# Attention ahead of two expert layers on one core: a per-engine order worked out in the source and chained, tiles 0 and 1 in one step, coefficients loaded later

## The chip, the cores and the metric

One core of a Trainium2 chip runs the whole program. The metric is the device time of one execution in microseconds (us). The engines are TensorE (PE, with PEld for its weight loads), VectorE (DVE), ScalarE (ACT), GpSimd (POOL) and SyncE (SP), which issues the loads and stores.

## What is computed

Causal attention for 2 batches and 12 heads over 448 tokens with heads of 64 wide, then an expert layer with a rational activation, then a gated one:

```python
def _attn_ref(q, k, v):
    ...
    scores = scale * np.matmul(q, k.transpose(0, 1, 3, 2))
    scores = np.where(mask, -1000000000.0, scores)
    scores = scores - np.max(scores, axis=-1, keepdims=True)
    attn = np.exp(scores)
    attn = attn / (np.sum(attn, axis=-1, keepdims=True) + 1e-09)
    return np.matmul(attn, v).astype(np.float32)

def _moe_ref(x, w_in, w_out, a, b):
    h = x @ w_in
    P = a[0] + a[1] * h + a[2] * h2 + a[3] * h3
    Q = 1.0 + np.abs(b[0]) * np.abs(h) + np.abs(b[1]) * h2
    g = P / (Q + 1e-06)
    return (g @ w_out).astype(np.float32)

def _moe2_ref(x, w_gate, w_val, w_out):
    gate = 1.0 / (1.0 + np.exp(-(x @ w_gate)))
    val = x @ w_val
    return (gate * val @ w_out).astype(np.float32)
```

x has 896 tokens (448 of each batch) by 768. w_in is 768 by 2048, w_out of the first layer 2048 by 768, the weights of the second 768 by 1536 and back. q, k and v are float32; the weights come as float64.

## The kernel before

**Attention.** Two heads of one batch make a pair, so there are 12 pairs, n = 0 to 11, 0 to 5 of batch 0. The 448 queries of a pair are four tiles t = 0 to 3 of 112 rows, and tile t meets t + 1 key tiles. For each tile: `scores` (L334) on PE for both heads into a PSUM slot "s"; `maxima` (L342) on VectorE masks, scales and takes the row maximum; `exps` (L358) on ScalarE; `turn` (L374) on PE transposes the exponentials into another slot "s" (called p); `copied` brings them to memory, on ScalarE for t = 2 (L381), else on VectorE (L383). At the pair's last tile `inverses` (L365, L366) inverts the row sums, `values` spreads them on PE (r, L395) and multiplies by v (x, L404), `result` (L416, L417) multiplies both, and `parts` splits the result into xh (L424, ScalarE) and xl (L427, GpSimd, or VectorE for the last pair of a batch). The pool of "s" has two slots, shared by s and p; x and r have one bank each, and two banks "mm" are left for the expert layer.

**Products of the expert layers.** Each product of full precision is three matmuls: high by high, high by low, low by high part. `weight` makes the parts of a weight: a load of 768 KB into "raw" (L117), two ScalarE steps (L126, L129), one VectorE step to "val" (L132), a ScalarE cast (L137, the high part) and a GpSimd subtraction (L139, the low part). raw and val have two buffers each. The first layer runs over four chunks of four tiles of 128 hidden values. h<c>_<b>_<i> is tile i of chunk c for batch b, 18 matmuls in `up` (L185, L187, L189); `rational` then makes its parts gh (L214, ScalarE) and gl (L216, GpSimd) by way of z, d and t (ScalarE L197 to L199, L207, L208; VectorE L201 to L203, L210 to L212). o<c>_<b>_<e> is tile e of the six output tiles, 12 matmuls in `out1` (L288, L290, L292), added into y by `sum1`.

**The order.** A loop over 48 steps (n, t) with a look-ahead of three (L474) emits the stages of attention, each at raised priority (`ahead`), and puts pieces of other work between them: two products each from a list of fillers (`products`), the steps of the first weights (`fetch`), and the rest of the rationals (`tick`). The framework's scheduler then fixes the order on each engine. h0_0_0 and h0_0_1 go in pair by pair as x gets ready (`early`), h0_0_2, h0_0_3 and o0_0 in the second half (`FILL_AT`). After attention its memory is released, and the chunks follow in a fixed sequence: h0_1, then for each chunk the next weights, next h and o. The loads of pairs 0 and 1, then those of the coefficients a and b, stand first on SP, and the negated b first on VectorE:

```python
    load(0)
    load(1)
    nc.sync.dma_start(out=a_sb, in_=ca.unsqueeze(0).to_broadcast([P, 4]))
    nc.sync.dma_start(out=b_sb, in_=cb.unsqueeze(0).to_broadcast([P, 2]))
    nc.vector.tensor_scalar_mul(nb, b_sb, -1.0)
    nc.vector.tensor_tensor(nb, nb, b_sb, op=ALU.min)
```

Of the kernel before, what the change touches and what calls it, by code (L numbers as in the profile page):

```python
# [26 lines left out]
def _run(g):  # L27
    while not _spent(g):
        pass


@with_exitstack
def tile_causal_attention__moe_rational__moe_glu(
# [74 lines left out]
    last = {}  # L108

    def paced(engine):  # L110

        return tc.issue_after(last[engine].ins) if engine in last else nullcontext()

    def weight(hi, lo, src, nm):
# [11 lines left out]
        nc.scalar.activation(w_f, w_f, AF.Prelu, scale=2.0**-112, alpha=2.0**32)  # L126

# [3 lines left out]
        with paced("dve"):  # L131
            nc.vector.scalar_tensor_tensor(  # L132
                val, w_hi, 3, w_lo, op0=ALU.logical_shift_left, op1=ALU.bitwise_or
            )
# [24 lines left out]
    NF = 4  # L159
# [32 lines left out]
    def rational(ps, gh, gl, nm):  # L192
# [12 lines left out]
        yield  # L205
# [30 lines left out]
    def early(k, after):  # L236

        for i in range(2):
            nm = f"h0_0_{i}"
            if k == 0:  # L240
                if i == 0:
                    gh = g_a.tile([P, 2, S], F32R, tag="gh", name=f"gh_{nm}")
                    gl = g_a.tile([P, 2, S], F32R, tag="gl", name=f"gl_{nm}")
                else:
                    gh, gl = g["e"]
                g["e"] = gh, gl
                g[0, 0, i] = (gh[:, i], gl[:, i])
                g["p", i] = psum_tile(nm)
            yield from up(g["p", i], wi[0][0], i * P, 0, [k])
            if k == KC - 1:  # L250
                after(rational(g["p", i], *g[0, 0, i], nm))

    def in1(c, b, after, i0=0):

        for i in range(i0, NF):
            nm = f"h{c}_{b}_{i}"
            if i % 2 == 0:
                pool = gpools[(c * B + b) % 2]
                gh = pool.tile([P, 2, S], F32R, tag="gh", name=f"gh_{nm}")
                gl = pool.tile([P, 2, S], F32R, tag="gl", name=f"gl_{nm}")  # L260
            g[c, b, i] = (gh[:, i % 2], gl[:, i % 2])
            ps = psum_tile(nm)
            yield from up(ps, wi[c][i // 2], (i % 2) * P, b)
            after(rational(ps, *g[c, b, i], nm))
# [14 lines left out]
    def out1(c, b, after):  # L279
        if c == 0:  # L280
            y1.append(ypools[b].tile([P, YW], F32, tag="y", name=f"y1_{b}"))
        for e in range(KC):
            es = slice(e * P, (e + 1) * P)
            ps = psum_tile(f"o{c}_{b}_{e}")
# [9 lines left out]
            after(sum1(ps, c, b, e))  # L294
# [7 lines left out]
    st = att.enter_context(tc.tile_pool(name="st", bufs=6))  # L302
# [5 lines left out]
    steps = [(n, t) for n in range(len(pairs)) for t in range(NQ)]  # L308
    T = {}

    PK = NQ - 1
    NB = PK * PK + NQ

    def load(n):
# [37 lines left out]

    def exps(n, t):
        d = T[n]
        sc = d["sc", t]
        for j in range(2):
            e = d["e", t, j]
            nc.scalar.activation(  # L358
                e, e, AF.Exp, bias=sc[:, j : j + 1], scale=-1.0, accum_out=d["sum"][:, t, j : j + 1]
            )  # L360

    def inverses(n, t):
        if t == NQ - 1:
# [21 lines left out]
    def values(n, t):  # L385

        if t < NQ - 1:
            return
        d = T[n]
        d["r"] = ps_r.tile([P, 512], F32, tag="r", name=f"r_{n}")[:, :S]  # L390
        d["x"] = ps_x.tile([P, 512], F32, tag="x", name=f"x_{n}")[:, :S]

        for i in range(NQ):
            for j in range(2):
# [6 lines left out]
                )  # L401
        for kt in range(NQ):
            for j in range(2):
                last["pe"] = nc.tensor.matmul(  # L404
                    d["x"][j * D : (j + 1) * D, kt * CP :],
                    d["v"][:, kt, j],
                    d["pt"][:, j, kt * (PK + 1) : kt * PK + NQ].rearrange("p k c -> p (k c)"),
                    start=(kt == 0),
                    stop=(kt == NQ - 1),
                )  # L410

    def result(n, t):
        if t == NQ - 1:
            d = T[n]
            xn = d["xn"] = xn_p.tile([P, S], F32, tag="xn", name=f"xn_{n}")
            nc.scalar.copy(xn, d["r"])  # L416
            nc.vector.tensor_tensor(xn, xn, d["x"], op=ALU.mult)  # L417

    def parts(n, t):
        if t == NQ - 1:  # L420
            b, hp = pairs[n]
            x = (slice(None), hp, slice(b * S, (b + 1) * S))
            xn = T[n]["xn"]
            nc.scalar.copy(xh[x], xn)  # L424

            eng = nc.vector if hp == NP - 1 else nc.gpsimd
            eng.tensor_tensor(xl[x], xn, xh[x], op=ALU.subtract)  # L427
            del T[n]

    side = []  # L430
    queue = deque()
    loading = []
    fill = deque()
    held = []

    def ahead(offset=50):
        return tc.high_priority(offset=offset)

    def tick():
        for s in list(side):  # L440
            if _spent(s):
                side.remove(s)

    def fetch():
        if not loading and queue:
            loading.append(queue.popleft())
        if loading and _spent(loading[0]):
            loading.clear()

    def products():  # L450
        with paced("pe"):
            k = 4 if held and fill and fill[0] is held[0] else 1
            while k > 0 and fill and not (held and fill[0] is held[0] and side):
                if _spent(fill[0]):
                    fill.popleft()
                else:
                    k -= 1

    def stage(f, i):
        if 0 <= i < len(steps):  # L460
            with ahead():
                f(*steps[i])

    ns = len(steps)
    LA = 3
    AHEAD = 4
    IN_AT, OUT_AT, FILL_AT = 4, 14, ns // 2 + 1
    load(0)
    load(1)
    nc.sync.dma_start(out=a_sb, in_=ca.unsqueeze(0).to_broadcast([P, 4]))  # L470
    nc.sync.dma_start(out=b_sb, in_=cb.unsqueeze(0).to_broadcast([P, 2]))
    nc.vector.tensor_scalar_mul(nb, b_sb, -1.0)
    nc.vector.tensor_tensor(nb, nb, b_sb, op=ALU.min)
    for i in range(-LA, ns + 1):  # L474
        m, off = divmod(i + LA + AHEAD, NQ)
        if off == 3 and 1 < m + 1 < len(pairs):
            load(m + 1)
        if i == IN_AT:
            queue.extend(load_in(0))

# [3 lines left out]
        if i == OUT_AT:  # L484
            queue.extend(load_out(0))
# [182 lines left out]
```

## Time and profile before

| what | value |
|---|---|
| median of 3 runs | 663.45 us (663.27 to 663.7) |
| the profiled execution, its own time | 663.94 us |
| its span, first to last instruction | 662.2 us |
| mean granted clock of PE, share of 2.4 GHz | 0.969 |
| busy: PE, PEld, DVE, ACT, POOL | 94%, 81%, 58%, 57%, 36% |
| loaded and stored | 65 MB, 97 GB/s over the span |

The profile is of one execution. An engine's busy share is a mean over stages that differ: attention, up to about 175 us, is made of many small steps on four engines, and what follows is mostly long runs of matmuls. So the stage is read first, and in it what PE waits for, since an engine that is idle without anyone waiting for it costs nothing. A row of the timeline gives start, duration, engine, line, written<-read tile, the number of instructions joined, and in brackets the idle time before it with what ended it. The names there leave out the numbers: "h" is any h tile.

### The profile page before, as it was taken

Reading aid. Unit: us, or ns where it says so; the run is one execution under the profiler, and the core shown is the slowest. Engines: PE = TensorE matmul, PEld = TensorE weight load, DVE = VectorE, ACT = ScalarE, POOL = GpSimd, SP = SyncE. Lnnn points to the kernel's source line nnn. Section 1 sums busy time; section 2 is a strip of 40 time slices with the busy share of each in tenths; the row PEclk is TensorE's granted clock in tenths of the full one; section 3 lists DMA queues with packets and bytes.
Section 4 is the critical chain, followed back from the end, with each engine's and each line's share of the span. In section 5 each row is a group of like instructions: output and inputs, shape, how many; then the busy total and the mean of one; then the engine's idle time right before and its main releaser. Section 6 shows DMA issues by size and latency. Waiting matters only on the chain.

```text
span 662.2 us, 8797 instructions
## 1 busy us (share of the span) xinstructions
PE 623.8 (94%) x3352; PEld 534.1 (81%) x3352; DVE 386.8 (58%) x659; ACT 380.0 (57%) x712; POOL 237.8 (36%) x155
## 2 busy tenths in 40 slices
PE   5888688999898999999999989999999999999997
PEld 3555355577697888999999879899999999999997
DVE  2656658843489899998978964222433454222314
ACT  3677878844397988869638848565544424310110
POOL 0132402110255464262245779433614334220100
PEclk7779979999998999999999989999999999999999
DMA  6262641100054155123006345352322504100004
GB/s 222 86 215 87 215 149 46 42 15 1 1 191 143 49 159 175 49 60 131 0 5 195 136 130 173 126 191 76 115 96 95 191 1 150 42 1 0 1 1 166
DMA packets 25641, 65.05 MB, mean 98 GB/s; under 512 B 1984, under 2 KB 3776, under 8 KB 25600
## 3 DMA queue, kind: packets, MB, share of 16 engines
q1 hardware_dynamic: 25600, 64.50, 29.7%
q8 instruction: 26, 0.43, 0.3%
q14 instruction: 15, 0.12, 0.1%
HBM read 61.74 MB, written 2.75 MB: 97 GB/s over the span
## 4 chain that ended last, share of the span: by engine, by line
PE 61%; DVE 15%; ACT 10%; issue 5%; DMA 4%; POOL 4%; SPq 0%; DVEq 0%; ACTq 0%; POOLq 0%
PE z L598 4%; PE z L599 4%; PE z L600 4%; PE vu L185 4%; PE gu L185 4%; PE gu L189 4%; PE vu L189 4%; PE gu L187 4%; PE vu L187 4%; PE s L334 3%; PE h L185 3%; PE p L374 3%; PE o L288 3%; PE h L187 3%; PE o L292 3%
## 5 line engine op out<-in xcount | busy, mean ns | idle before, releaser
L185 PE MATMUL h<-xh,wh_in 128*128 128x448 f32 x192 | 71.4, 377 | 6.8 <-ACT xh L424 5.0
L288 PE MATMUL o<-gh_h,oh 128*128 128x448 f32 x192 | 69.2, 377 | 5.7 <-DVE t_h L203 3.9
L586 POOL TENSOR_TENSOR gl<-pr_u,gh 128x448 fp32r<-128x448 f32 x24 | 28.4, 1183 | 127.0 <-ACT gh L585 127.0
L290 PE MATMUL o<-gl_h,oh 128*128 128x448 f32 x192 | 72.2, 376 | 1.5 <-POOL gl_h L216 1.4
L187 PE MATMUL h<-xl,wh_in 128*128 128x448 f32 x192 | 71.5, 373 | 1.5 <-POOL xl L427 1.5
L292 PE MATMUL o<-gh_h,ol 128*128 128x448 f32 x192 | 71.4, 372 | 0.0
L189 PE MATMUL h<-xh,wl_in 128*128 128x448 f32 x192 | 70.8, 370 | 0.0
L216 POOL TENSOR_TENSOR gl_h<-t_h,gh_h 128x448 fp32r<-128x448 f32 x32 | 45.1, 1412 | 61.9 <-ACT gh_h L214 48.7
L358 ACT ACTIVATE e<-e,sc 112x112 f32<-112x112 f32 (+3 forms) x96 | 50.0, 524 | 28.9 <-DVE sc L342 28.8
L342 DVE CUSTOM_DVE_ANT_0 e<-s,mask 112x112 f32<-112x112 f32 (+3 forms) x96 | 39.1, 446 | 33.8 <-PE s L334 33.2
L582 DVE TENSOR_TENSOR pr_u<-sg_u,vu 128x448 f32<-128x448 f32 x24 | 14.8, 617 | 73.3 <-PE vu L189 54.5
L598 PE MATMUL z<-oh_z,gh 128*128 128x384 f32 x168 | 56.3, 335 | 0.0
L599 PE MATMUL z<-ol_z,gh 128*128 128x384 f32 x168 | 56.2, 334 | 0.0
L600 PE MATMUL z<-oh_z,gl 128*128 128x384 f32 x168 | 56.2, 334 | 0.0
L185 PE MATMUL gu<-xh,wh_gt 128*128 128x448 f32 x144 | 53.0, 368 | 0.7 <-ACT sg_u L581 0.7
L185 PE MATMUL vu<-xh,wh_vl 128*128 128x448 f32 x144 | 53.1, 369 | 0.0
L189 PE MATMUL vu<-xh,wl_vl 128*128 128x448 f32 x144 | 53.0, 368 | 0.0
L187 PE MATMUL vu<-xl,wh_vl 128*128 128x448 f32 x144 | 53.0, 368 | 0.0
L187 PE MATMUL gu<-xl,wh_gt 128*128 128x448 f32 x144 | 53.0, 368 | 0.0
L189 PE MATMUL gu<-xh,wl_gt 128*128 128x448 f32 x144 | 53.0, 368 | 0.0
L427 POOL TENSOR_TENSOR xl<-xn,xh 128x448 fp32r<-128x448 f32 x10 | 12.8, 1277 | 110.8 <-ACT xh L424 110.8
L605 DVE TENSOR_TENSOR y<-y,z 128x384 f32<-128x384 f32 x70 | 37.8, 551 | 23.1 <-PE z L600 23.1
(93 smaller groups left out, 1529.4 us busy)
## 6 DMA issues: line engine op xcount, KB each, us to landing
raw_in<-in_moe_w_in_dram SPq DMA_DIRECT2D x16, 768.0 KB, 4.8
raw<-in_moe_w_out_dram SPq DMA_DIRECT2D x16, 768.0 KB, 4.2
raw_gt<-in_moe_w_gate_dram SPq DMA_DIRECT2D x12, 768.0 KB, 4.4
raw_vl<-in_moe_w_val_dram SPq DMA_DIRECT2D x12, 768.0 KB, 4.4
raw_z<-in_moe_w_out_dram SPq DMA_DIRECT2D x12, 768.0 KB, 4.4
qk<-in_qk_dram SPq DMA_DIRECT2D x12, 448.0 KB, 4.0
v<-in_v_dram SPq DMA_DIRECT2D x12, 224.0 KB, 3.0
out_dram<-y SPq DMA_DIRECT2D x14, 192.0 KB, 1.8
```

The lines of the kernel that those rows point to most:

```text
L185: nc.tensor.matmul(ps, hi[:, c, fs], xh[:, c, bs], start=(c == 0), stop=False)
L187: nc.tensor.matmul(ps, hi[:, c, fs], xl[:, c, bs], start=False, stop=False)
L189: nc.tensor.matmul(ps, lo[:, c, fs], xh[:, c, bs], start=False, stop=(c == KC - 1))
L216: nc.gpsimd.tensor_tensor(gl, t, gh, op=ALU.subtract)
L288: nc.tensor.matmul(ps, hi[:, es], gh, start=(i == 0), stop=False)
L290: nc.tensor.matmul(ps, hi[:, es], gl, start=False, stop=False)
L292: nc.tensor.matmul(ps, lo[:, es], gh, start=False, stop=(i == NF - 1))
L342: last["dve"] = nc.vector.tensor_tensor_reduce(e, d["s", t][:, j], mask[:, S - nk :], op0=ALU.add, op1=ALU.min, scale=SCALE, scalar=3.0e38 ...
L358: nc.scalar.activation(e, e, AF.Exp, bias=sc[:, j : j + 1], scale=-1.0, accum_out=d["sum"][:, t, j : j + 1])
L598: nc.tensor.matmul(ps, gh[:, ms], hi[:, ns], start=(i == 0), stop=False)
L599: nc.tensor.matmul(ps, gh[:, ms], lo[:, ns], start=False, stop=False)
L600: nc.tensor.matmul(ps, gl[:, ms], hi[:, ns], start=False, stop=(i == NF2 - 1))
```

## The change

The loop over steps, its fillers and the priorities go. In their place every group of instructions of the attention, of the first chunk's weights, of h0_0 and of o0_0 is a `Job` with an engine, an estimated cost, the jobs it depends on, and a rank. `in_turn` walks through time: on the engine that is free first it takes, of the jobs that are ready, the one of lowest rank. The jobs are emitted in this order, and every instruction is tied to the one before it on its engine, with an order-only dependency. Tiles 0 and 1 of a pair are one step: their scores stand in one slot "s", and so do their transposes, so that a pair has three steps. The maxima of a pair lie in one tile `sc`. The values are four jobs, one for each key tile. h0_0_2, h0_0_3 and o0_0 have rank 1000, the last choice. The loads of a and b come behind the load of pair 2 and a first weight load, the negated b on VectorE behind the maxima of pairs 0 and 1. `weight` has one more stop, `rational` one less. What follows attention is written as before.

```diff
+def in_turn(jobs, handoff):
...
+    for _ in jobs:
+        now, e = min((max(free[e], min(j.ready for j in w)), e) for e, w in waiting.items() if w)
+        job = min((j for j in waiting[e] if j.ready <= now), key=lambda j: j.rank)
+        waiting[e].remove(job)
+        free[e] = now + job.cost
...
+        yield job
...
-    steps = [(n, t) for n in range(len(pairs)) for t in range(NQ)]
+    GROUPS = [(0, 1), (2,), (3,)]
...
+    def scores(n, k):
 
         d = T[n]
...
+        ps = d["s", k] = ps_s.tile([CP, 2, 512], F32, tag="s", name=f"s_{n}_{k}")
+        for t in GROUPS[k]:
+            o, nk = cols_of(t)
+            c = slice(t * CP, (t + 1) * CP)
+            for j in range(2):
+                r = slice(j * D, (j + 1) * D)
+                nc.tensor.matmul(
+                    ps[:, j, o : o + nk], d["qk"][r, 0, c], d["qk"][r, 1, :nk], start=True, stop=True
+                )
...
-    load(0)
-    load(1)
-    nc.sync.dma_start(out=a_sb, in_=ca.unsqueeze(0).to_broadcast([P, 4]))
-    nc.sync.dma_start(out=b_sb, in_=cb.unsqueeze(0).to_broadcast([P, 2]))
-    nc.vector.tensor_scalar_mul(nb, b_sb, -1.0)
-    nc.vector.tensor_tensor(nb, nb, b_sb, op=ALU.min)
-    for i in range(-LA, ns + 1):
...
+    R_TURN, R_R, R_X, R_W = -6, -3, 22, 0
+    R_MAX, R_COPY, R_INV, R_XN = -4, 1.5, 0.5, 8
+    R_EXP, R_ROUT = 0.75, -14
...
+            for t in GROUPS[k]:
+                for j in both:
+                    job(("max", n, t, j), "DVE", MAX[t] + 0.08, [("s", n, k), ("p", n - 1, k)], rank + R_MAX, maximum, n, k, t, j)
+                    job(("exp", n, t, j), "ACT", EXP[t] + 0.19, [("max", n, t, j), ("r", n - 3)], rank + R_EXP, exponentials, n, t, j)
...
+    job("ab", "SP", 2.0, [("load", 2)], 4, coefficients)
+    job("nb", "DVE", 0.32, ["ab"], 20, negated)
...
+    for n in range(NP):
+        for i in range(2):
+            matmuls(("h", i), n, [*done[: n_in // 2], ("lo", n)], in1_tile, (0, 0, i))
...
+    for i in range(2, NF):
+        deps = [*done[:n_in], *freed_by("mm")]
+        for u in range(KC):
+            matmuls(("h", i), u, deps, in1_tile, (0, 0, i))
+        h_follows(i)
+    for e in range(KC):
+        deps = [*done, ("h after", NF - 1, len(AFTER) - 1), *freed_by("mm")]
+        for u in range(NF):
+            matmuls(("y", e), u, deps, out1_tile, (0, 0, e))
...
+    for j in in_turn(jobs, {"PE": 0.2, "DVE": 0.1, "ACT": 0.12, "POOL": 0.12, "SP": 0.1}):
...
+        j.emit()
+        for ins in traced[before:]:
+            if ins.engine in latest:
+                tc.add_manual_dep(
+                    ins,
+                    latest[ins.engine].name,
+                    mybir.DependencyInfo(mybir.DependencyClass.NoSync, mybir.DependencyReason.DATA),
+                    reason="in turn",
                 )
...
     att.close()
```

A row of the order lists below is a line of the source, an operation, written<-read tiles with a number of their own behind each, and the shape. x_11 is the value product of pair 11, s_n_k and p_n_k the scores and transposes, e_n_t_j the exponentials.

VectorE at the start of the program, before:

```order
L80 MEMSET ones_83 128x256
L472 TENSOR_SCALAR nb_114<-b_sb_113 128x2
L342 ISA e_0_0_0_163,sc_0_0_162<-s_0_0_159,mask_107 112x112
L342 ISA sc_0_0_162 112x1
L342 ISA e_0_1_0_173,sc_0_1_172<-s_0_1_169,mask_107 112x224
```

and with the change, its first rows, and those around the negated b at place 39:

```order
L114 MEMSET ones_83 128x256
L373 ISA e_0_0_0_177,sc_0_0_160<-s_0_0_169,mask_107 112x112
L373 ISA sc_0_0_160 112x1
L373 ISA e_0_0_1_179,sc_0_0_160<-s_0_0_169,mask_107 112x112
L373 ISA sc_0_0_160 112x1
```

```order
L373 ISA sc_0_1_167 112x1
L415 COPY pt_0_0_161<-p_0_2_272 112x2x4x112
L548 TENSOR_SCALAR nb_114<-b_sb_113 128x2
L549 TENSOR_TENSOR nb_114<-nb_114,b_sb_113 128x2
L373 ISA e_2_0_0_307,sc_0_2_198<-s_2_0_292,mask_107 112x112
```

The negated b, nb, has moved from ahead of the first maximum to behind the maxima of pair 1 and the first copies.

PE around the end of attention, before:

```order
L374 MATMUL p_11_2_1599<-ident_102,e_11_2_0_1548 112x112 x3
L374 MATMUL p_11_2_1599<-ident_102,e_11_2_1_1550 112x112 x3
L374 MATMUL p_11_3_1607<-ident_102,e_11_3_0_1580 112x112 x4
L374 MATMUL p_11_3_1607<-ident_102,e_11_3_1_1582 112x112 x4
L395 MATMUL r_11_1617<-ident_102,sum_1_5_1298 64x112 x8
L404 MATMUL x_11_1618<-pt_1_5_1299,v_1_5_1296 64x448 x2
L404 MATMUL x_11_1618<-pt_1_5_1299,v_1_5_1296 64x336 x2
L404 MATMUL x_11_1618<-pt_1_5_1299,v_1_5_1296 64x224 x2
L404 MATMUL x_11_1618<-pt_1_5_1299,v_1_5_1296 64x112 x2
L185 MATMUL h0_1_1_1697<-xh_117,wh_in0_0_293 128x448
L187 MATMUL h0_1_1_1697<-xl_118,wh_in0_0_293 128x448
L189 MATMUL h0_1_1_1697<-xh_117,wl_in0_0_294 128x448
```

and with the change:

```order
L213 MATMUL h0_0_3_1399<-xh_117,wh_in0_2_145 128x448
L215 MATMUL h0_0_3_1399<-xl_118,wh_in0_2_145 128x448
L217 MATMUL h0_0_3_1399<-xh_117,wl_in0_2_146 128x448
L442 MATMUL x_11_1457<-pt_1_5_1183,v_1_5_1179 64x448 x2
L442 MATMUL x_11_1457<-pt_1_5_1183,v_1_5_1179 64x336 x2
L442 MATMUL x_11_1457<-pt_1_5_1183,v_1_5_1179 64x224 x2
L442 MATMUL x_11_1457<-pt_1_5_1183,v_1_5_1179 64x112 x2
L305 MATMUL o0_0_0_1496<-gh_h0_0_0_499,oh_0_0_147 128x448
L307 MATMUL o0_0_0_1496<-gl_h0_0_0_500,oh_0_0_147 128x448
L309 MATMUL o0_0_0_1496<-gh_h0_0_0_499,ol_0_0_148 128x448
```

Before, the products of batch 1 (h0_1) begin ahead of pair 11's end, and o0_0 is done. With the change h0_0 fills up to the end, and o0_0 and all of h0_1 stand behind it.

PE where the products of o0_1 begin, with the change (the last products of h0_1_0, the first and the last of h1_0_3's 18):

```order
L213 MATMUL h0_1_0_1602<-xh_117,wh_in0_0_143 128x448
L215 MATMUL h0_1_0_1602<-xl_118,wh_in0_0_143 128x448
L217 MATMUL h0_1_0_1602<-xh_117,wl_in0_0_144 128x448
L213 MATMUL h1_0_3_1889<-xh_117,wh_in1_2_1746 128x448
L215 MATMUL h1_0_3_1889<-xl_118,wh_in1_2_1746 128x448
L217 MATMUL h1_0_3_1889<-xh_117,wl_in1_2_1747 128x448
...
L215 MATMUL h1_0_3_1889<-xl_118,wh_in1_2_1746 128x448
L217 MATMUL h1_0_3_1889<-xh_117,wl_in1_2_1747 128x448
L305 MATMUL o0_1_0_1925<-gh_h0_1_0_1600,oh_0_0_147 128x448
```

There h0_1_0 ends 18 products ahead of o0_1; before, it ended some 90 ahead. ScalarE around gh of h0_1_0, before:

```order
L207 ACTIVATE d_h0_1_1_1718<-z_h0_1_1_1717,one_115 128x448
L208 ACTIVATE d_h0_1_0_1683<-d_h0_1_0_1683 128x448
L126 ACTIVATE raw_in2_0_3_2225<-raw_in2_0_3_2225 128x768
L129 ACTIVATE raw_in2_0_3_2225<-raw_in2_0_3_2225 128x768
L208 ACTIVATE d_h0_1_1_1718<-d_h0_1_1_1718 128x448
L137 CAST wh_in2_0_2213<-val_in2_0_0_2219 128x768
L214 CAST gh_h0_1_0_1660<-t_h0_1_0_1681 128x448
L197 ACTIVATE z_h0_1_2_1754<-h0_1_2_1734 128x448
```

and with the change:

```order
L234 ACTIVATE d_h0_1_0_1623<-z_h0_1_0_1622,one_115 128x448
L235 ACTIVATE d_h0_1_0_1623<-d_h0_1_0_1623 128x448
L234 ACTIVATE d_h0_1_1_1658<-z_h0_1_1_1657,one_115 128x448
L235 ACTIVATE d_h0_1_1_1658<-d_h0_1_1_1658 128x448
L154 ACTIVATE raw_1_2_2213<-raw_1_2_2213 128x768
L158 ACTIVATE raw_1_2_2213<-raw_1_2_2213 128x768
L154 ACTIVATE raw_1_3_2221<-raw_1_3_2221 128x768
L158 ACTIVATE raw_1_3_2221<-raw_1_3_2221 128x768
L241 CAST gh_h0_1_0_1600<-t_h0_1_0_1621 128x448
L225 ACTIVATE z_h0_1_2_1694<-h0_1_2_1674 128x448
```

The cast of gh (L214 before, L241 with the change) stood behind the conversion of two weights of w_in for chunk 2, and now stands behind that of two weights of w_out for chunk 1, raw_1_2 and raw_1_3. VectorE makes the values that free their buffers here:

```order
L160 SCALAR_TENSOR_TENSOR val_in2_2_3_2183<-raw_in2_2_3_2181 128x768
L229 SCALAR_TENSOR_TENSOR z_h0_1_0_1622<-z_h0_1_0_1622,nb_114,d_h0_1_0_1623 128x448
L160 SCALAR_TENSOR_TENSOR val_1_0_2199<-raw_1_0_2197 128x768
L230 TENSOR_TENSOR t_h0_1_0_1621<-t_h0_1_0_1621,h0_1_0_1602 128x448
L229 SCALAR_TENSOR_TENSOR z_h0_1_1_1657<-z_h0_1_1_1657,nb_114,d_h0_1_1_1658 128x448
L160 SCALAR_TENSOR_TENSOR val_1_1_2207<-raw_1_1_2205 128x768
```

val_1_0 and val_1_1 stand behind z of h0_1_0, so behind the end of its products.

## Rows read from the trace of the kernel before

**Rows 1.** The page: busy us and share; PE and its clock in 40 slices

```profile
PE 623.8 (94%) x3352; PEld 534.1 (81%) x3352; DVE 386.8 (58%) x659; ACT 380.0 (57%) x712; POOL 237.8 (36%) x155
...
PE   5888688999898999999999989999999999999997
...
PEclk7779979999998999999999989999999999999999
```

**Rows 2.** Timeline of PE at pair 11's end and at the first o0_1

```profile
173.07 2.11 PE L404 MATMUL x<-pt,v 112*64 112x448 f32 x16 [0.31 <-issue]
...
203.82 0.37 PE L292 MATMUL o<-gh_h,ol 128*128 128x448 f32 x1
...
205.65 0.36 PE L292 MATMUL o<-gh_h,ol 128*128 128x448 f32 x1
209.24 0.74 PE L288 MATMUL o<-gh_h,oh 128*128 128x448 f32 x1 [3.23 <-DVE t_h L203]
209.78 0.57 PE L290 MATMUL o<-gl_h,oh 128*128 128x448 f32 x1
...
216.35 0.47 PE L290 MATMUL o<-gl_h,oh 128*128 128x448 f32 x1 [0.78 <-POOL gl_h L216]
```

**Rows 3.** Busy time by window: length, engines (instructions), clock, DMA share, GB/s

```profile
130.34:148.11 17.77, 17.77 (x114) 12.88 (x113) 8.93 (x30) 9.64 (x28) 2.27 (x2) 1.00 0.05 14
```

**Rows 4.** Groups by line on PE in that window: busy us, mean ns, idle before

```profile
L290 PE MATMUL o<-gl_h,oh 128*128 128x448 f32 x15 | 5.8, 383 | 0.0
```

**Rows 5.** Timeline of the start, all engines

```profile
3.05 0.43 SPq L471 DMA_DIRECT2D b_sb<-in_moe_b_dram  x1
...
4.72 0.84 PE L334 MATMUL s<-qk 64*112 64x112 f32 x8
10.06 0.17 DVE L472 TENSOR_SCALAR nb<-b_sb 128x2 f32<-128x2 f32 x1 [8.93 <-DMA b_sb<-in_moe_b_dram]
...
11.04 1.46 PE L334 MATMUL s<-qk 64*112 64x336 f32 x4 [5.48 <-DVE sc L342]
...
12.43 0.62 PE L374 MATMUL p<-ident,e 112*112 112x112 f32 x2
```

**Rows 6.** What PE waited for up to 176 us: total, times, longest (10 kinds)

```profile
PE s L334 <- DVE sc L342: 7.8, 5, 5.5
PE p L374 <- DVE pt L383: 6.7, 9, 1.8
```

**Rows 7.** Busy time by window: 28 to 31.75, and the four windows at half clock

```profile
28.00:31.75 3.75, 1.61 (x15) 1.15 (x14) 3.67 (x13) 3.10 (x9) 1.51 (x2) 1.00 0.64 189
...
7.85:24.92 17.07, 13.03 (x58) 7.24 (x58) 7.23 (x32) 10.47 (x30) 0.00 (x0) 0.50 0.47 159
...
sum 34.12, PE 28.62 PEld 17.73 DVE 15.07 ACT 23.59 POOL 5.25; mean PE 7.16 PEld 4.43 DVE 3.77 ACT 5.90 POOL 1.31
```

**Rows 8.** Busy time by window: the whole attention, and ten us of it

```profile
0.00:175.20 175.20, 150.24 (x991) 96.42 (x991) 98.89 (x301) 113.93 (x290) 33.50 (x31) 0.90 0.32 102
110.00:120.00 10.00, 9.07 (x70) 5.92 (x70) 8.41 (x27) 9.30 (x25) 3.61 (x3) 1.00 0.19 58
```

**Rows 9.** Durations by line, ns min/median/max and first, last start; a load, us

```profile
L137 ACT CAST wh_in<-val_in x16: 814/832/869, 30.5 to 256.1; 128x768 fp32r<-128x768 f32 x16
L198 ACT ACTIVATE d_h<-h,b_sb x32: 606/628/719, 99.1 to 369.1; 128x448 f32<-128x448 f32 x32
L201 DVE SCALAR_TENSOR_TENSOR z_h<-z_h,nb,d_h x32: 633/686/2276, 99.8 to 370.9; 128x448 f32<-128x448 f32 x32
L132 DVE SCALAR_TENSOR_TENSOR val<-raw x16: 919/950/2607, 61.9 to 345.8; 128x768 uint32<-128x768 uint32 x16
L129 ACT ACTIVATE raw<-raw x16: 882/904/934, 46.0 to 311.5; 128x768 uint32<-128x768 uint32 x16
L216 POOL TENSOR_TENSOR gl_h<-t_h,gh_h x32: 1137/1284/1894, 112.3 to 385.9; 128x448 fp32r<-128x448 f32 x32
raw<-in_moe_w_out_dram SPq DMA_DIRECT2D x16, 768.0 KB, 4.2
```

More of the change, by code (lines that the diff above doesn't have):

```diff
@@ L29, in _run, with __init__ @@
         pass
+class Job:
+    def __init__(self, engine, cost, deps, rank, emit):
+        self.engine, self.cost, self.rank, self.emit = engine, cost, rank, emit
+        self.deps = [d for d in deps if d is not None]
+        self.waits = len(self.deps)
+        self.ready = 0.0
+        self.then = []
+        for d in self.deps:
+            d.then.append(self)
+def in_turn(jobs, handoff):
+    free = {}
+    waiting = {}
+    for j in jobs:
+        free.setdefault(j.engine, 0.0)
+        waiting.setdefault(j.engine, [])
+        if not j.waits:
+            waiting[j.engine].append(j)
+    for _ in jobs:
[3 more added lines that the diff above has]
+        free[e] = now + job.cost
+        for j in job.then:
+            j.ready = max(j.ready, free[e] + (handoff[e] if j.engine != e else 0.0))
+            j.waits -= 1
+            if not j.waits:
+                waiting[j.engine].append(j)
+        yield job
 @with_exitstack
@@ L234, in load_out, with in1_tile, in1 @@
         return todo
[L236 to L264, printed above, removed]
+    def in1_tile(c, b, i):
+        nm = f"h{c}_{b}_{i}"
+        if i % 2 == 0:
+            pool = gpools[(c * B + b) % 2]
+            gh = pool.tile([P, 2, S], F32R, tag="gh", name=f"gh_{nm}")
+            gl = pool.tile([P, 2, S], F32R, tag="gl", name=f"gl_{nm}")
+            g["t", c, b, i // 2] = gh, gl
+        gh, gl = g["t", c, b, i // 2]
+        g[c, b, i] = (gh[:, i % 2], gl[:, i % 2])
+        ps = psum_tile(nm)
+        return up(ps, wi[c][i // 2], (i % 2) * P, b), rational(ps, *g[c, b, i], nm)
+    def in1(c, b):
+        for i in range(NF):
+            for w in in1_tile(c, b, i):
+                _run(w)
     def sum1(ps, c, b, e):
@@ L293, in out1 @@
                 yield
-            after(sum1(ps, c, b, e))
+        return products(), sum1(ps, c, b, e)
+    def out1(c, b):
+        for e in range(KC):
+            for w in out1_tile(c, b, e):
+                _run(w)
     att = ExitStack()
@@ L419, in parts @@
[L419 to L457, printed above, removed]
@@ L511, in tile_causal_attention__moe_rational__moe_glu, with factors_out, values @@
-    att.close()
-    last.clear()
-    while side or loading or queue:
-        tick()
-        fetch()
-    for f in fill:
-        _run(f)
+    def factors_out(n):
+        T[n]["xn"] = xn_p.tile([P, S], F32, tag="xn", name=f"xn_{n}")
+        nc.scalar.copy(T[n]["xn"], T[n]["r"])
+    def values(n, kt):
+        d = T[n]
+        if kt == 0:
+            d["x"] = ps_x.tile([P, 512], F32, tag="x", name=f"x_{n}")[:, :S]
+        for j in range(2):
+            nc.tensor.matmul(
+                d["x"][j * D : (j + 1) * D, kt * CP :],
+                d["v"][:, kt, j],
+                d["pt"][:, j, kt * (PK + 1) : kt * PK + NQ].rearrange("p k c -> p (k c)"),
+                start=(kt == 0),
+                stop=(kt == NQ - 1),
+            )
@@ new lines, in tile_causal_attention__moe_rational__moe_glu @@
+    portions = load_in(0)
+    n_in = len(portions)
+    portions += load_out(0)
+    for p, w in enumerate(portions):
+        for m, (engine, cost) in enumerate(STAGES):
+            deps = [("w", p, m - 1) if m else ("load", 1)]
+            deps.append({0: ("w", p - 2, 3), 3: ("w", p - 2, 5)}.get(m))
+            rank = W_AT + W_STEP * p + (-4 if m == 0 else R_W)
+            job(("w", p, m), engine, cost, deps, rank, _spent, w)
+    done = [("w", p, len(STAGES) - 1) for p in range(len(portions))]
@@ new lines, in tile_causal_attention__moe_rational__moe_glu, with products, follow, matmuls @@
+    tiles = {}
+    def products(key, make, args):
+        if key not in tiles:
+            tiles[key] = make(*args)
+        for _ in range(3):
+            next(tiles[key][0])
+    def follow(key):
+        _spent(tiles[key][1])
+    AFTER = [("ACT", 1.7), ("DVE", 1.86), ("ACT", 1.2), ("DVE", 1.86), ("ACT", 0.6), ("POOL", 1.3)]
+    unit = None
+    def matmuls(key, u, deps, make, args):
+        nonlocal unit
+        job((key, u), "PE", 0.56, [unit, *deps], 1000, products, key, make, args)
+        unit = (key, u)
```

270 lines of the change are left out of this document (147 added, 123 removed).

## The prediction, made before the changed kernel ran

> **What bounds the kernel now.** I read the busy shares and the 40 slices first [rows 1]: the matrix engine PE is busy 94% of the span, and of the slices below 9 the first seven and the eleventh lie in the attention, the thirteenth right behind it. The granted clock is low there too. So the span is PE's work plus what PE loses, and a change of order can only give back losses. The end of the attention is the last value product of pair 11, which starts at 173.07 [rows 2] and ends at about 175.2.
>
> How much of these 175.2 us is work? Between the value products of pairs 8 and 9, from 130.34 to 148.11, PE is busy all 17.77 us at full clock [rows 3]. In that stretch lie one pair's scores, transposes, factors and values, and 45 MoE products (15 on L290 [rows 4], as many on L288 and L292). MoE products follow each other every 0.203 us: from the start at 203.82 to that at 205.65 are nine steps [rows 2]. 45 of them are 9.1 us, so **one pair is 8.64 us**, with its switching between forms. Twelve pairs are 103.7 us, and the 159 products that the old order puts ahead of the end (72 h0_0, 72 o0_0, 15 h0_1) are 32.3 us. With the first score product at 4.72 [rows 5] that makes 140.7; the attention loses the other **34.5 us**.
>
> Where? PE's waits up to 176 us add to 25.7 us; the two largest kinds are 7.8 us of scores behind maxima, 5.5 of it in one piece, and 6.7 of transposes behind copies [rows 6]. And in four stretches, 34.1 us in all, the granted clock is 0.50, the 1.2 GHz level, while PE is busy 28.6 us [rows 7]; half of that, 14.3 us, is lost. Together 40.0, 5.5 more than the sum leaves, so 8.64 us per pair is rather too much than too little.
>
> **The change, part by part.**
>
> *Coefficients later.* b_sb is issued at 3.05 and the first vector work, nb on L472, stands idle 8.93 us for it until 10.06; the maxima queue behind it, and PE stands 5.48 us until 11.04 [rows 5]. In the new order the maxima are first on VectorE and nb is at place 39, behind the maxima of pairs 0 and 1, when b_sb has long landed (about 10 us even in the old trace). On SP the two loads stand behind a weight load. Nobody needs b_sb or nb before the first rational. The wait goes entirely. What is late next is the ordinary start: the maxima follow nb at 10.06, and the first transposes start at 12.43 [rows 5], 2.4 us in which two PSUM slots let PE run little else. I take 2.3 us for this once.
>
> *o0_0 and the first h0_1 products leave the attention.* The new order has 72 products (h0_0) ahead of the end instead of 159. 72 x 0.203 = 14.6 us. The other 87 are not saved: they stand behind the end and are counted below.
>
> *Tiles 0 and 1 share a step.* The same matmuls, transposes and maxima, with fewer changes of form and a slot handed over six times per pair instead of eight. I price this at nothing and set it against small waits that stay.
>
> *Every engine's order chained.* No instruction is added. What the chain can do is put a wait in front of ready work. I followed one mid pair by hand, with the durations of the trace, and found PE dense with six h0_0 products per pair to fill. ScalarE is the closest other engine: 113.9 us busy up to 175.2, less six y copies that move out, each about as long as a step of L198 (0.63 us [rows 9]), is 110.1 us, 87% of the new stretch. That cover is thin. VectorE has 98.9 [rows 8].
>
> *The clock.* In the old trace the low clock begins at 7.85, inside the 5.48 us idle, and holds to 24.92 although PE is busy 13.0 of 17.1 us [rows 7]; before the other three PE had stood still for some 2 us each, the first time busy 1.61 of 3.75 us [rows 7]. With the idle gone I count one dip: 3.23 us idle before 209.24 were followed by products of 0.57 instead of 0.36 us and 0.37 instead of 0.20 apart, up to 212.65 [rows 2], about 1.7 us lost. The Trainium skill, page "TensorE: Matmul & The Clock Gate", section "What's actually happening", says that the default state is throttled and activity releases the throttle. The old trace agrees at 7.85 and 209.24. By that rule the first three pairs, which have no products to fill with in the new order either, could stay at 1.2 GHz, which gives a T near 153 instead of 127; that is rival C.
>
> *End of the attention.* T = 4.72 + 103.7 + 14.6 + 2.3 + 1.7 = **127.0 us**, against 175.2.
>
> *Behind T, up to the common place.* From the first product on gl of h0_1_2 on (216.35 in the old trace, "o <- gl_h" after 0.78 us of idle [rows 2]) both orders are the same on every engine. In the new one 198 products follow T: o0_0 72, h0_1 72, h1_0_0 to h1_0_2 54. 198 x 0.203 = 40.2 us, which I take as dense because the y copies free each slot some us ahead. Call their end E = T + 40.2; the last of them are h0_1_0, which in the old order was finished some 90 products earlier.
>
> *The new wait.* The next o0_1 products need gh of h0_1_0, and only the 18 products of h1_0_3 (3.7 us) stand between. In ScalarE's order the cast of that gh stands behind the conversion of raw_1_2 and raw_1_3, whose loads wait until VectorE has made val_1_0 and val_1_1, and these stand behind z of h0_1_0. The chain from E, with durations of [rows 9]: two casts of 0.83, z and d as L198, with handoffs E + 3.0; on VectorE z, val_1_0, t, z, val_1_1, the short ones 0.69 each; the load 4.2; the conversion two steps of 0.90. A val alone takes 0.95 us, and up to 2.61 with GpSimd at work [rows 9], whose two wl run just then: I take 1.8 for the first and 0.95 for the second. That is E + 13.8, and PE stands about 10 us. Both vals at 0.95 give 13.0, both at 2.6 give 16.3. Then 13 more ScalarE steps of some 0.63 (8.2) and a gl of 1.28 on GpSimd, with handoffs 9.7, lead to the common place; 7.1 in the old trace (209.24 to 216.35 [rows 2]) is the least. So the common place is at T + 40.2 + 13.8 + 9.7 = T + 63.7 = **190.7**, against 216.35: **25.7 us earlier**.
>
> *From there on* order, loads and engine places are the same, so the rest of 446 us is moved, not changed. I price it at nothing, give or take 3 us for loads that start against other work.
>
> **Sum.** The profiled execution took 663.94 (span 662.2 and 1.7 around it). 663.94 - 25.7 = 638.2; the median of the runs shown is 0.5 below that execution, so I predict **637.7 us**.
>
> **Rivals.**
>
> *A, the new wait is covered.* If gh of h0_1_0 is ready when PE arrives, the common place is at T + 244 x 0.203 (the 198, the 18 of h1_0_3 and 28 of o0_1) = T + 49.5 = 176.5, 39.8 earlier: 623.6 us. For it speaks that the old order's idle here is only 3.23 + 0.78 [rows 2]; against it that val_1_0 can't come before h0_1_0 ends, by the order. Chance 0.08; a wait of half the size gives about 630.
>
> *B, the attention stays loose.* The routine's costs are constants; an engine that is late drags a chain with it, and ScalarE at 87% has little to give. In the old trace one stretch of 10 us has ScalarE 9.3 busy and PE 9.07 [rows 8]. If six tenths of the 34.5 us stay (20.7), T = 143.7, the common place is 9.0 earlier: 654.4 us. Chance 0.15, spread over T from 138 to 151.
>
> *C, slower: the clock stays low in the early pairs.* The first MoE product stands among the work of pairs 2 and 3, so pairs 0 to 2 run on their own work. At 1.2 GHz they take twice 8.64 us. With the 2.3 us of start and another 5 us of waits, T = 123.0 + 25.9 + 7.3 = 156.2, and the new wait outweighs what is left: +3.5, 666.9 us. It decides from T = 152.8 on, that is 29.8 us lost in the attention. For it: the clock rows [rows 7]. Against: each old dip begins beside an idle stretch of PE, and the longest of those goes. Chance 0.06.
>
> *D, the order is not the one written.* The chains bind the attention, but its last part is interleaved by the scheduler. A kernel that keeps the old timing, or where B and the new wait cancel, lies within 0.2% (1.3 us, about what a measurement of this kernel can tell from no change): 0.03.
>
> The forecast itself keeps 0.68, with its own range 629 to 648 (T from 121 to 134, the chain's bounds and the 3 us later). **Range 625 to 656**: it leaves out more than half of A, the upper half of B, C and D, some 2 in 10. Faster 0.91, same 0.03, slower 0.06.
>
> **What would show it.** Right: no vector idle for b_sb, first maximum near 5 us; pair 11's last value product near 125; full clock in most slices there; one idle of about 10 us on PE some 44 us later, in front of an "o <- gh_h" row, with ScalarE converting raw just before; then the same 446 us. Wrong: value products over 11 us apart with waits for exponentials (B); a clock of 0.5 through the first 50 us (C); no idle at the o0_1 products (A); any stretch behind the common place that is longer than before.

## The result, and the profile after

The changed kernel takes 644.66 us (median of 4 runs, 644.05 to 646.85), the kernel before 663.36 beside it: ratio 0.9725, 95% interval 0.9701 to 0.975, 18.7 us less. The forecast was 637.7 with a range of 625 to 656. The profiled execution took 644.05 us with a span of 642.1.

The page of the changed kernel, its busy shares and the 40 slices of PE and of its clock (before: [rows 1]):

```profile
PE 611.5 (95%) x3352; PEld 527.1 (82%) x3352; DVE 377.7 (59%) x659; ACT 379.8 (59%) x712; POOL 233.3 (36%) x155
...
PE   7999998999749999999999899999999999999997
...
PEclk9999999999968999999999999999999999999999
```

The first eight slices are the attention now, and its clock is full in every one. The gap has moved: PE falls in slices 11 and 12, and the clock in 12 and 13. The timeline of PE shows both ends (before: [rows 2] and [rows 5]); "s" are scores, "p" transposes, "x" the value products, "o" products of w_out:

```profile
4.90 2.33 PE L365 MATMUL s<-qk 64*112 64x112 f32 x12
7.69 1.69 PE L365 MATMUL s<-qk 64*112 64x448 f32 x12 [0.46 <-DVE sc L373]
10.07 0.76 PE L405 MATMUL p<-ident,e 112*112 112x112 f32 x6 [0.69 <-DVE sc L373]
...
123.76 2.11 PE L442 MATMUL x<-pt,v 112*64 112x448 f32 x16
...
148.28 0.47 PE L305 MATMUL o<-gh_h,oh 128*128 128x448 f32 x1 [0.36 <-ACT y L284]
...
158.19 0.47 PE L305 MATMUL o<-gh_h,oh 128*128 128x448 f32 x1 [1.08 <-ACT y L284]
...
184.14 1.12 PE L305 MATMUL o<-gh_h,oh 128*128 128x448 f32 x2 [11.57 <-ACT gh_h L241]
...
193.34 1.08 PE L305 MATMUL o<-gh_h,oh 128*128 128x448 f32 x4 [2.03 <-ACT gh_h L241]
194.56 0.74 PE L307 MATMUL o<-gl_h,oh 128*128 128x448 f32 x1
```

The 5.48 us of idle at the start have become 0.46. Pair 11 ends at 125.9 instead of 175.2. Then PE stands 11.57 us for a gh, and the first product on gl of h0_1_2, the common place, starts at 194.56 instead of 216.35. Busy time by window for these stretches (length, then PE, PEld, DVE, ACT, POOL, clock, DMA share, GB/s; before: [rows 8]):

```profile
0.00:125.87 125.87, 117.33 (x904) 72.26 (x904) 93.55 (x292) 105.85 (x278) 29.92 (x29) 1.00 0.44 142
125.87:168.80 42.93, 41.15 (x199) 37.03 (x200) 16.19 (x18) 21.82 (x33) 14.38 (x8) 1.00 0.34 111
168.80:194.56 25.76, 11.92 (x47) 9.15 (x45) 18.04 (x27) 18.33 (x32) 7.51 (x5) 0.80 0.18 61
...
194.56:642.10 447.54, 441.07 (x2204) 408.70 (x2204) 249.95 (x324) 233.84 (x372) 181.46 (x113) 0.99 0.28 91
```

So the attention gives 49.3 us, the passage takes 27.5 of them back (68.7 us against 41.15, 17.7 of it the 87 products that moved there), and the rest is 1.7 longer (447.54 against 445.85). Together 20.1 us of span.

What PE waits for in the passage is seen on ScalarE and VectorE, from the end of h0_1_0's products at 168.75 on:

```profile
168.75 1.57 ACT L165 CAST wh_in<-val_in 128x768 fp32r<-128x768 f32 x2 [4.73 <-PE h L215]
...
178.79 0.90 ACT L154 ACTIVATE raw<-raw 128x768 f32<-128x768 f32 x1 [1.86 <-DMA raw<-in_moe_w_out_dram]
...
181.99 0.88 ACT L154 ACTIVATE raw<-raw 128x768 f32<-128x768 f32 x1 [1.52 <-DMA raw<-in_moe_w_out_dram]
...
183.54 0.55 ACT L241 CAST gh_h<-t_h 128x448 fp32r<-128x448 f32 x1
...
192.72 0.56 ACT L241 CAST gh_h<-t_h 128x448 fp32r<-128x448 f32 x1 [2.97 <-DVE t_h L239]
```

```profile
171.92 2.57 DVE L160 SCALAR_TENSOR_TENSOR val<-raw 128x768 uint32<-128x768 uint32 x1
...
175.54 0.95 DVE L160 SCALAR_TENSOR_TENSOR val<-raw 128x768 uint32<-128x768 uint32 x1
```

This is the foretold chain: casts, z, val_1_0, val_1_1, two loads, two conversions that each wait for a load, and only then the cast that PE stands for.

### The profile page after: what moved, and what is told of

The parts are those of the page before. It is cut to its first block, busy times and chain, and to the rows that moved or that the text cites. A ratio compares the mean times of both kernels' runs of the same rounds, so it can differ in the third digit from the quotient of the medians.

```text
span 642.1 us, 8794 instructions
## 1 busy us (share of the span) xinstructions
PE 611.5 (95%) x3352; PEld 527.1 (82%) x3352; DVE 377.7 (59%) x659; ACT 379.8 (59%) x712; POOL 233.3 (36%) x155
## 4 chain that ended last, share of the span: by engine, by line
PE 67%; DVE 14%; ACT 9%; DMA 6%; issue 3%; POOL 1%; DVEq 0%; ACTq 0%; POOLq 0%; SPq 0%
PE vu L213 5%; PE vu L215 5%; PE vu L217 5%; PE z L708 5%; PE z L710 5%; PE z L709 5%; PE gu L213 5%; PE gu L215 5%; PE gu L217 5%; PE o L307 3%; PE o L309 3%; PE s L365 3%; DMA raw<-in_moe_w_out_dram 3%; PE o L305 3%; PE p L405 3%
## 5 line engine op out<-in xcount | busy, mean ns | idle before, releaser
L243 POOL TENSOR_TENSOR gl_h<-t_h,gh_h 128x448 fp32r<-128x448 f32 x32 | 42.5, 1327 | 85.2 <-ACT gh_h L241 69.4
L215 PE MATMUL h<-xl,wh_in 128*128 128x448 f32 x192 | 70.2, 366 | 0.0
L167 POOL TENSOR_TENSOR wl_in<-val_in,wh_in 128x768 fp32r<-128x768 f32 x16 | 31.0, 1944 | 74.6 <-ACT wh_in L165 74.6
L692 DVE TENSOR_TENSOR pr_u<-sg_u,vu 128x448 f32<-128x448 f32 x24 | 14.8, 617 | 72.4 <-PE vu L217 53.8
L305 PEld LDWEIGHTS o<-gh_h,oh 128*128 128x128 f32 x192 | 36.7, 193 | 23.7 <-ACT gh_h L241 15.8
```

Of the source, the lines that this page charges most:

```text
L215: nc.tensor.matmul(ps, hi[:, c, fs], xl[:, c, bs], start=False, stop=False)
L243: nc.gpsimd.tensor_tensor(gl, t, gh, op=ALU.subtract)
```

## The experiments

**The coefficients, undone and alone.** Undone in the changed kernel, with every other engine's order kept:

```diff
-    for j in in_turn(jobs, ...):
+    order = list(in_turn(jobs, ...))
+    for key in ("nb", "ab"):
+        order.remove(J[key])
+        order.insert(order.index(J["load", 1]) + 1, J[key])
+    for j in order:
```

> The changed kernel with one thing undone: the loads of a and b stand again behind the load of pair 1, and the negated b first on VectorE; every other engine keeps its order. If the start wait is a loss by itself and the rest of the gain is the order's (my account), the first maxima slip by 5 to 6 us and, with the low clock behind the idle start, pair 11 ends 5.5 to 12 us later: 650 to 657 us. If the coefficients were most of the gain (rival), nearly all of the 19 us is lost: 659 or more.

Measured: 650.42 us, ratio to before 0.9818 (0.9788 to 0.9847), so 5.8 us more than the changed kernel. The negated b waits again, and PE behind it (timeline), and the clock falls (busy time by window):

```profile
10.30 0.17 DVE L548 TENSOR_SCALAR nb<-b_sb 128x2 f32<-128x2 f32 x1 [9.17 <-DMA b_sb<-in_moe_b_dram]
...
11.79 2.96 PE L365 MATMUL s<-qk 64*112 64x448 f32 x12 [4.38 <-DVE sc L373]
```

```profile
10.00:15.00 5.00, 2.96 (x12) 1.48 (x13) 3.44 (x18) 3.55 (x14) 0.00 (x0) 0.56 1.00 345
15.00:20.00 5.00, 4.40 (x20) 2.80 (x22) 3.14 (x15) 2.85 (x13) 0.00 (x0) 0.50 0.07 28
```

Pair 11 ends at 134.0, 8.1 us later, and time and place are inside what was foretold. The longer idle, 4.38 us instead of 0.46, is half of the 8.1 us, and the half clock that begins in it, 10.6 to 20.9, the other half. The same part put into the kernel before:

```diff
-    nc.sync.dma_start(out=a_sb, ...)   
-    nc.sync.dma_start(out=b_sb, ...)
-    nc.vector.tensor_scalar_mul(nb, b_sb, -1.0)
-    nc.vector.tensor_tensor(nb, nb, b_sb, op=ALU.min)
     for i in range(-LA, ns + 1):
...
+        if i == 1:
+            nc.sync.dma_start(out=a_sb, ...)
+            nc.sync.dma_start(out=b_sb, ...)
+        if i == 6:
+            with paced("dve"):
+                nc.vector.tensor_scalar_mul(nb, b_sb, -1.0)
+                nc.vector.tensor_tensor(nb, nb, b_sb, op=ALU.min)
```

> The kernel before with that one part of the change alone: a and b are loaded behind pair 2, the negated b behind the second pair's maxima. My account: 5.5 us of start and part of the 6.5 us of half clock up to 24.92 go, the later waits and dips stay: 651 to 658 us. Rival (the coefficients are most of the gain): 648 or less.

Measured: 660.25 us, ratio 0.9968 (0.9948 to 0.9988), 2.6 us less. Neither account held. The idle at the start is gone, but the clock falls all the same, at 11.3 us, behind three idles of 0.7 to 1.0 us, and then the old order finds its next long wait: PE stands 2.45 us for the sums.

```profile
16.18 1.76 PE L395 MATMUL r<-ident,sum 112*64 112x112 f32 x16 [2.45 <-DVE sum L366]
```

```profile
10.00:20.00 10.00, 6.63 (x40) 4.99 (x42) 3.00 (x16) 7.21 (x18) 0.00 (x0) 0.56 0.48 183
```

Pair 0's values start 3.5 us earlier, at 21.5 instead of 25.0, and pair 11 ends 2.8 earlier. The part is worth 2.6 us in the old order and 5.8 in the new one. Why the new order keeps more of it was not tried.

**Four steps per pair.**

```diff
-    GROUPS = [(0, 1), (2,), (3,)]
+    GROUPS = [(0,), (1,), (2,), (3,)]
```

> The changed kernel with four steps per pair, so tiles 0 and 1 have a slot each again, in the same routine (look-ahead of three steps). If the shared step is worth nothing by itself (my price), pair 11 ends within 2 us of 125.9 and the time is 643 to 647. If the slots handed over eight times per pair bind (rival), pairs stretch by 0.3 to 0.7 us each: 648 to 653.

Measured: 640.15 us, ratio 0.9678 (0.9635 to 0.9721), below both forecasts, while pair 11 ends at 136.0, ten us *later*. The edit changed two things: behind the attention the framework's scheduler let h0_1_0 end 94 products ahead of o0_1 instead of 18, so that the wait there is 2.6 us instead of 11.6:

```profile
PE o L305 <- ACT gh_h L241: 2.6, 1, 2.6
```

(what PE waited for: total, times, longest). The steps had to be compared with the same passage, which the next experiment gives.

**The other bank.** The first h tile behind the attention takes a bank that o0_0 still holds. Shifting the count by one gives it another:

```diff
-    nmm = [0]
+    nmm = [1]
```

> The changed kernel, with the count that deals out the PSUM banks behind the attention shifted by one, so that h0_1_0 takes one of the six banks that attention gives back instead of one of the two that o0_0 still holds. It then stands right behind pair 11 on PE, and val_1_0 no longer waits for it. If the 11.6 us of idle before o0_1 come from h0_1_0's late slot (my account), they go almost whole, and with them the two low stretches of the clock behind: 629 to 635 us. If the conversion of raw_1_2 and raw_1_3 in front of the cast is late for itself (rival), the idle stays at 8 us or more: 641 to 645.

Measured: 626.06 us, ratio 0.9462 (0.943 to 0.9494), 18.6 us less than the changed kernel and more than my account asked for. Page and waits from 120 to 240 us:

```profile
PE 605.5 (97%) x3352; PEld 524.0 (84%) x3352; DVE 388.9 (62%) x659; ACT 378.1 (61%) x712; POOL 235.6 (38%) x155
...
PEclk9999999999999999999999999999999999999999
```

```profile
PE o L305 <- ACT gh_h L241: 1.4, 1, 1.4
```

The wait of 13.6 us in two pieces is down to 1.4, the two waits for y copies are gone, and the clock is full from end to end. On PE, h0_1_0 now ends 119 products ahead of o0_1. The two profiled spans differ by 17.7 us (642.1 and 624.4): PE is idle 11.7 us less, and busy 6.0 less, which is nearly all time at half clock (177.5 to 187.8, 194.6 to 198.0 and 368.7 to 372.1 in the changed kernel, about 5 us together). The shift gives every later tile another bank as well, so this is the price of the whole dealing, not of the one tile alone. Run again:

> The kernel of e5_other_bank once more, beside the one above on the same chip: 624 to 629 us if the gain holds on another day, over 632 if that run was a lucky one.

Measured: 626.02 us, ratio 0.9437 (0.9412 to 0.9462). This version beats both kernels, the one before by 37 us. In this profile the clock is not full from end to end:

```profile
106.81:110.22 3.41, 3.40 (x13) 1.94 (x11) 1.99 (x4) 3.41 (x9) 0.00 (x0) 0.50 0.00 0
```

**The cast ahead of the conversions.** Was it the late slot, or the conversions in front of the cast?

```diff
+        return tc.issue_after(mark["h0_1_1"].ins) if nm in ("1_2", "1_3") else nullcontext()
...
+        with after_cast(nm):
+            nc.scalar.activation(w_f, w_f, AF.Prelu, scale=2.0**-112, alpha=2.0**32)
...
+        with after_cast(nm):
+            nc.scalar.activation(w_lo, w_lo, AF.Copy, scale=2.0**-29 * (1 - EPS), bias=7.5 * EPS - 0.5)
...
+        mark[nm] = nc.scalar.copy(gh, t)
```

> The changed kernel, with the ScalarE conversions of raw_1_2 and raw_1_3 placed behind the casts of gh of h0_1_0 and h0_1_1 instead of ahead of them; PE keeps its order. If the late slot of h0_1_0 sets the idle (my account after e5), its t is ready at about 180.5 whatever ScalarE converts, so the idle falls from 11.6 to about 8.6 only: 641 to 643 us. If the conversions waiting for their loads are the cause (rival), it falls to 5 or less: 636 to 639.

Measured: 644.74 us, ratio 0.9714 (0.9679 to 0.9749): no gain, and outside both forecasts. Timeline of PE, and the cast on ScalarE:

```profile
182.30 1.11 PE L313 MATMUL o<-gh_h,oh 128*128 128x448 f32 x2 [8.61 <-ACT gh_h L249]
...
189.83 0.47 PE L313 MATMUL o<-gh_h,oh 128*128 128x448 f32 x1 [1.78 <-DVE t_h L239]
194.60 1.53 PE L313 MATMUL o<-gh_h,oh 128*128 128x448 f32 x4 [2.04 <-ACT gh_h L249]
```

```profile
181.68 0.57 ACT L249 CAST gh_h<-t_h 128x448 fp32r<-128x448 f32 x1 [3.63 <-DVE t_h L247]
```

The idle falls to 8.61, as foretold: ScalarE stands 3.63 us for t, so the conversions were the last 3 us of the wait, and the rest is the late slot with the chain behind it. The time was not foretold, since the 3 us are lost again at once: from 184.5 to 187.7 the conversions now stand ahead of the next rational's steps, PE waits 1.78 more there, and the next group starts at 194.60, no earlier than the 193.34 of the changed kernel.

**Four steps per pair, with the other bank**, and the same with a longer lead (LA = 4):

> The kernel of e5_other_bank with four steps per pair instead of three, look-ahead of three steps, so that nothing but the steps differs from it. If the 10 us by which pair 11 ended later in e3_single_tiles are the price of single steps (what that trace suggests), 632 to 638 us. If they came from elsewhere in its order (rival), 624 to 629.

> The same with a look-ahead of four steps, a whole pair, as the three steps of the changed kernel are. If the loss of single steps is the shorter lead (theory 1), it vanishes: 624 to 629 us. If it is the number of hand-overs of the two slots (theory 2), it stays: 632 to 640.

Measured: 638.85 us, ratio 0.9621 (0.9585 to 0.9658), and 642.75, ratio 0.9681 (0.9629 to 0.9734). The first is 0.9 us above its range for the price of single steps, the second above both of its ranges. Against 626.06 the single steps cost 12.8 us, and the longer lead doesn't give them back. Pair 11 ends at 136.8 and 138.0, against 126.3. Busy time of e7 by window, with its two stretches at half clock, then of e5 up to its pair 11:

```profile
0.00:136.80 136.80, 125.18 (x908) 76.76 (x909) 98.40 (x301) 109.90 (x284) 33.36 (x31) 0.96 0.40 131
...
95.00:100.00 5.00, 3.49 (x24) 2.20 (x22) 3.32 (x5) 4.94 (x11) 1.81 (x1) 1.00 0.16 46
100.00:105.00 5.00, 3.80 (x17) 2.76 (x17) 4.93 (x16) 3.73 (x11) 1.58 (x1) 0.59 0.50 161
...
100.89:107.72 6.83, 6.52 (x37) 4.89 (x38) 5.26 (x17) 5.29 (x14) 1.58 (x1) 0.50 0.33 110
131.61:135.02 3.41, 3.41 (x21) 2.09 (x19) 0.65 (x1) 0.53 (x1) 0.65 (x1) 0.50 0.00 0
```

```profile
0.00:126.30 126.30, 117.81 (x904) 72.22 (x904) 93.59 (x292) 105.90 (x278) 29.97 (x29) 1.00 0.43 141
```

The work is the same but for three products of o0_0; PE is busy 7.4 us longer and idle 3.1 us longer. Half of the 9.93 us that it is busy in the two stretches at half clock, 5.0 us, is lost to the clock; the first of them begins in a wait of 2.7 us for a maximum that ends at 101.2, the second behind waits of 0.8, 1.2 and 1.2 in the last pair. So at most 2.4 of the 7.4 us can be those products and the changes of form. Behind pair 11 another half-clock stretch (189.6 to 193.1) costs 1.7. That it isn't the lead is shown; that it is the number of hand-overs is not.

**The ties.** The version with the other bank, the jobs emitted in the same order, without the dependency of each instruction on the one before:

```diff
-            if ins.engine in latest:
-                tc.add_manual_dep(ins, latest[ins.engine].name, ..., reason="in turn")
```

> The kernel of e5_other_bank (626 us) without the dependencies that tie each instruction to the one before it on its engine: the jobs are emitted in the same order, and the framework's scheduler is free to reorder. If the pinned order is what removed the waits (my account), pair 11 ends 10 to 30 us later and the time is 635 to 655. If the emitted order alone does it (rival), 624 to 629.

Measured: 651.41 us, ratio 0.9808 (0.9783 to 0.9832): 25 us lost. Pair 11 ends at 156.4, 30 us later, but half of that is no loss: the 72 products of o0_0 stand ahead of it there (976 instructions of PE instead of 904). Timeline:

```profile
13.27 0.17 DVE L548 TENSOR_SCALAR nb<-b_sb 128x2 f32<-128x2 f32 x1 [3.76 <-DMA b_sb<-in_moe_b_dram]
...
14.70 1.47 PE L365 MATMUL s<-qk 64*112 64x336 f32 x4 [4.28 <-DVE sc L373]
```

The scheduler draws the negated b from place 39 to 18, where it waits again. One tie put back, for that step alone (`if ins.engine in latest and j is J["nb"]:`):

> The kernel of e4_unchained (651 us) with one tie put back: the negated b stays behind the instruction ahead of it in the routine's order, all else is free. In the trace of e4_unchained the scheduler had drawn it ahead of pair 1's maxima, VectorE stood 3.76 us for the load, and PE 4.28. If this one move is most of what the ties prevent (rival), the time falls to 630 or less. If it is worth what the coefficients were in e1_coef_first and the ties earn the rest in many small places (my account), 643 to 647 us.

Measured: 649.45 us, ratio 0.9794 (0.9759 to 0.9829). So putting it back gives 2 us, less than either forecast, and the other 23 are elsewhere. As in e2, the next wait comes up once this one is gone:

```profile
15.78 1.76 PE L424 MATMUL r<-ident,sum 112*64 112x112 f32 x16 [2.52 <-DVE sum L394]
```

The free scheduler also draws the weights forward: from 20 to 60 us ScalarE and GpSimd (the fourth and fifth numbers) are fuller in e9 than in e5, shown below it.

```profile
20.00:40.00 20.00, 15.57 (x135) 9.92 (x134) 15.98 (x47) 19.85 (x42) 9.68 (x7) 0.99 0.78 266
40.00:60.00 20.00, 19.07 (x127) 10.86 (x127) 14.44 (x41) 19.02 (x48) 8.53 (x5) 0.92 0.67 217
```

```profile
20.00:40.00 20.00, 19.59 (x162) 11.62 (x160) 16.31 (x51) 17.60 (x47) 5.89 (x4) 1.00 0.52 168
40.00:60.00 20.00, 20.00 (x172) 12.79 (x170) 15.36 (x48) 16.79 (x46) 6.56 (x5) 1.00 0.53 176
```

In these 40 us ScalarE runs 27 conversions and casts of weights in e9 and 12 in e5, and PE is busy 4 us less in the first 20. That these conversions are the cause was not tried.

## Why the prediction was right

The direction, the mechanism and the place of the new wait held, and the time is in the range; the gain is 18.7 us where 25.7 were forecast. Step by step, in the profiled execution:

| step | forecast, us | measured, us |
|---|---|---|
| end of the attention T | 127.0 | 125.9 |
| T to the end of h0_1_0 | 40.2 | 42.9 |
| from there to the cast of gh | 13.8 | 14.8 |
| to the common place | 9.7 | 11.0 |
| behind it, against before | 0 | +1.7 |

The errors add to 5.6 us: 25.7 less 5.6 is the 20.1 of the spans. That T came within 1.1 us is in part luck, as the third point shows.

- *Coefficients later* was right: the idle of 5.48 is 0.46, and undoing it costs 5.8 us. The start then loses 3.0 us in five small waits up to 18 us, where I took 2.3; the first two are 0.46 and 0.69.
- *The clock* was too dear: I counted one dip of 1.7 us in the attention and there is none. Rival C did not come; the early pairs run at full clock. The rule of the Trainium skill ("TensorE: Matmul & The Clock Gate", "What's actually happening") that activity releases the throttle agrees with this, and with the drop when b_sb is waited for again (0.56 and 0.50 in e1). It was a near thing: in e9, with idles of 0.77, 0.69 and 0.72 us at the start where the changed kernel has 0.46, 0.69 and 0.72, the clock falls at 12.3.
- *Tiles 0 and 1 share a step* was the step that failed: priced at nothing, it is worth 12.8 us with the bank of e5 on both sides, of which 3.1 are waits in the attention and 6.7 half clock. The sum did not show it, because the price of a pair, 8.64 us, came from the old order with four steps and was too high for the new one, and the waits that I counted were too low: PE's waits between the first scores and pair 11's end add to 6.7 us (its two largest kinds are shown below) where I had 2.3, and (125.9 - 4.9 - 14.6 - 6.7) / 12 gives 8.3 us per pair. Two errors met. My own cross-check was closer than I read it: the 25.7 us of old waits hold 1.2 us ahead of the first scores and 0.8 behind pair 11, so the sum was 3.5 us too high, not 5.5, and that is 0.3 us per pair. What PE waited for up to 140 us (total, times, longest; before: [rows 6]):

```profile
PE s L365 <- DVE sc L373: 2.4, 4, 0.9
PE p L405 <- ACT e L387: 1.7, 3, 0.8
```

- *Every engine's order chained*: the ties are worth 25 us with the other bank. My hand-followed pair was right: PE is busy 10.0 of 10 us from 40 to 90.
- *Behind T* I took the 198 products as dense because the y copies would be ahead. Two were not, 1.4 us, and the first product behind T waited 0.3 us for a t step of VectorE. With these PE is idle 1.8 of the 42.9 us; the other 0.9 of the 2.7 us I can't place.
- *The new wait* was mis-sized by one term: val_1_0 took 2.57 us, the upper bound, where I took 1.8. The common place then came late by another cause than mine: not 13 steps of ScalarE, but VectorE's t, for which the cast at 192.72 waited 2.97 us.
- *From there on nothing* left out that the clock falls once more behind the 2.03 us of idle that end at 193.34: products start 0.37 apart instead of 0.20 from 194.56 to about 198, which is the 1.7.

Rival A, the wait covered, was priced at 623.6 us; with the other bank, which covers it, the time is 626.06. So the wait is where the forecast put it, but its price was too low: 14.1 us lie between forecast and rival A, 18.6 between the two kernels. The half clock behind the wait was not in the sum.

## What to carry to other kernels

Here an order worked out ahead kept most of its gain only while it was pinned: the same jobs in the same emission order lost 25 of 37 us when the scheduler could draw later work forward. A pinned stretch ends somewhere, and what is behind inherits its state: here one PSUM bank still held at the seam pushed a tile some 160 places back, and one number that deals the banks out differently was worth 18.6 of 37 us. And a step whose work is the same is not for that reason free: a pair with three steps instead of four was worth 12.8 us, about half of it time at half clock, behind waits that the version with three steps does not have.

## What the runs showed of the hardware that was not expected

PE's clock stayed full through the first 20 us of the changed kernel although PE was busy only 15.7 of them; it fell in the kernel with the coefficients first, where one idle was 4.38 us long, and in the changed kernel during an idle of 11.57 and behind one of 2.03 us. But short idles do not keep it up for certain: in e2 it fell behind idles of 0.7 to 1.0 us, and of two executions of one kernel, both with PE idles of 0.8 and 0.6 us between 104 and 108 us, e10 had half clock from 106.81 to 110.22 and e5 full clock. A VectorE step with both inputs in memory, 0.95 us alone, took 2.57 while GpSimd made two wl (4.01 us from 169.66), and the next one of the same size, begun at 175.54 when they were done, 0.95 again. All 13 such steps of the changed kernel that took over 2.5 us ran beside a GpSimd step.
